# Turning the first pairs' queries and keys at another place in the order of an attention and expert kernel

## The chip, the cores and the metric

One core of a Trainium2 chip runs the whole program. The metric is the device time in microseconds of one execution; the kernel before takes 1123.53 us, the median of three runs that lie between 1121.69 and 1123.55 us. Beside these there is one profiled execution with its trace.

## The reference

Attention with a block causal mask (blocks of 64) over 8 batches, 8 heads, 576 rows and head width 64 is followed by a gated two-layer network on all 4608 rows:

```
scores = scale * (q @ k.T);  scores = where(block_i >= block_j, scores, -1e9)
attn   = exp(scores - max);  attn = attn / (sum + 1e-9);  x = attn @ v
h = x @ w_in                         # 512 -> 2048
out = (h * sigmoid(1.702 * h)) @ w_out   # 2048 -> 512
```

## The kernel before

The attention works on pairs of heads: 32 pairs, four for each batch. The heads of one pair lie on the two halves of the 128 partitions. For each pair a *turn* (`step(n)`) goes through a written list of items, one slot after the other:

- a number such as `1+0`, `2/3` or `4` computes the scores of these row chunks (`score`): matrix products into PSUM banks, then on the vector engine (DVE) a masked minimum at line 351, on the scalar engine (ACT) the exponential with its sum at line 358, then the small DVE operations at lines 368 and 371 (sum plus epsilon, reciprocal), and on GpSimd (POOL) the scaling at line 376;
- `B`, `C` and `a` (`flip`) transpose the scaled weights through the matrix engine (PE, line 102) into a PSUM bank, from which ACT copies them (lines 411 and 424);
- `V` (`av`) multiplies them with the values, and ACT copies the result into `xr` (lines 451 and 450);
- `L` (`prep(n+1)`) turns the queries and the keys of the next pair: two DVE transposes (line 297) from `raw` into `qk`, one of the queries (x = 0) and one of the keys (x = 1), after which `load` issues the eight transfers of a later pair's queries and keys (the one after the next, so that `prep(2)` issues the load of pair 4) on the queue of SP (line 279).

Four pairs form a phase. Turns 0 to 3 use `ORDER[0]`, turn 4 uses `START`, turns 5 to 7 `ORDER[1]` and the rest `ORDER[2]`.

The experts' weights come in 32 pieces of 128 x 512 numbers, split in two by `convert`, which runs a little further after each slot. A piece passes over ACT (line 219), three times over DVE (lines 223, 229, 234), then ACT (line 243) and POOL (line 82); a piece's first ACT step stands behind the last DVE step of the piece before. Its words are loaded by SP (line 202). When the four pairs of the first batch are through, the experts begin on tiles of 384 rows, and from there their matrix products (`hp`, `acc`) are mixed with the attention of later pairs.

The instructions of PE stand in the order in which the program wrote them (`keep_in_program_order`). On the other engines and on the transfer queues a planner in the framework makes the order ahead of time, from its own estimates of durations and landings: where several instructions of an engine are ready by these estimates, the one with the smallest number goes first, and numbers count up in the order of the program. `tc.high_priority(offset=300)` takes 300 from the number. On the chip each engine runs its list in this fixed order and waits at an instruction whose inputs are not there.

A PSUM bank is taken in rotation: until the experts begin there are seven of them, and one turn of the first phase takes 21. The second group of transposes of `B` thus falls on the bank that the last `V` filled, and must wait for the copy at line 451.

Of the kernel before, what the change touches and what calls it, by code (L numbers as in the profile page):

```python
# [23 lines left out]


ORDER = (
# [3 lines left out]
)  # L30
# [10 lines left out]
def attention_moe_kernel(  # L41
# [9 lines left out]
    nc = tc.nc  # L51
    B, H, S, D = q.shape
# [11 lines left out]
    HP = H // 2  # L64
# [9 lines left out]
    def early(n):  # L74

        return n < 2 * HP
# [185 lines left out]
    raw, qk = {}, {}  # L262
# [5 lines left out]
    def load(n):  # L268

        if n in (1, 3):  # L270
            raw[n] = room("xh", [P, 2, S // 32, 32], F32, "raw")
        else:
            raw[n] = d2.tile([P, 2, S // 32, 32], F32, tag="raw", name="raw", bufs=1)
        for x, src in enumerate((q, k)):
            queue = nc.scalar if n < 2 and x else nc.sync
            for hd, b, h in heads(n):
                for c in range(0, D, 32):
                    r = hd * D + c
                    queue.dma_start(
                        out=raw[n][r : r + 32, x],  # L280
                        in_=src[b, h][:, c : c + 32].rearrange("(c p) d -> p c d", p=32),
                    )
# [9 lines left out]
    def prep(n):  # L292

        tag = "e0" if early(n) and n % 2 else "qk"
        qk[n] = d2.tile([P, 2, S], F32, tag=tag, name="qk", bufs=1)
        for x in range(2):
            nc.vector.transpose(out=qk[n][:, x], in_=raw[n][:, x].rearrange("p c d -> p (c d)"))  # L297
        raw.pop(n)
        m = follower(n)
        if m is not None:  # L300
            load(m)
# [154 lines left out]
    def follower(n):  # L456

        m = {0: 2, 1: 3, 2: 4, 3: None}.get(n, n + 1)
        return None if m is None or m >= NPAIR else m
# [4 lines left out]
    def step(n):  # L464

        turns["n"] = n
        now = n < NPAIR

        def item(x):
            if x == "V":  # L470
                return (lambda: av(n - 1)) if n else None
            if x == "L":
                return (lambda: prep(n + 1)) if n + 1 < NPAIR else None
            if x in ("a", "B", "C"):
                m, chunks = {"a": (n, [0, 1]), "B": (n - 1, [2, 3]), "C": (n - 1, [4])}[x]
                return (lambda: flip(m, chunks)) if m >= 0 else None
            return (lambda: score(n, [[int(z) for z in y.split("+")] for y in x.split("/")])) if now and x != "-" else None

        return [item(x) for x in order(n)]
# [139 lines left out]
    load_weights(2)  # L619
    load_v(0)  # L620
    prep(0)
    load_v(1)
    heads_done = 0
# [41 lines left out]
```

## Time and profile before

| | |
|---|---|
| median of three runs | 1123.53 us (1121.69 to 1123.55) |
| profiled execution | 1120.49 us |
| its span, first to last instruction | 1118.6 us |
| mean granted clock of the matrix engine | 0.992 of full speed |
| matrix engine busy over the span | 96% |
| vector engine, scalar engine, GpSimd busy | 52%, 45%, 36% |

The profiled execution is 1.89 us longer than its span and 3.04 us shorter than the median. The busy shares are means over stages that differ: the first 77 us hold the attention of the first batch and the first weights, the rest the experts beside the attention.

### The profile page before, as it was taken

What the parts mean: (1) busy time and instruction counts of PE and PEld (TensorE: products, weight loads), DVE (VectorE), ACT (ScalarE), POOL (GpSimd) and SP (SyncE); (2) the same over time, 40 slices, a digit from 0 to 9 for tenths busy, and PEclk for the clock granted to TensorE, in tenths of its full rate; (3) what the DMA queues carried; (4) which work ended last, traced back from release to release, by engine and by line L of the source; (5) the groups of instructions that cost most, each with busy time, mean ns of one, the idle gap of its engine ahead of it and who ended that gap; (6) DMA issues with size and microseconds to landing.
All of it is one profiled execution on the core that took longest, in us unless ns stands there. A gap on an engine that the chain in (4) does not pass through costs nothing. (4 is left out here: it accounts for less than half of the span.)

```text
span 1118.6 us, 19977 instructions
## 1 busy us (share of the span) xinstructions
PE 1076.4 (96%) x6960; PEld 908.7 (81%) x6960; DVE 583.0 (52%) x1856; ACT 498.6 (45%) x1321; POOL 406.7 (36%) x509
## 2 busy tenths in 40 slices
PE   5969998999999999999999999999999999999998
PEld 3757776788888888888888888888888888899997
DVE  6776885545545555654555655645545654211210
ACT  5866776434534433534443543444434444322322
POOL 4665664333333332333333333333333233122222
PEclk9979999999999999999999999999999999999999
DMA  8734532332444432343443333344342332200000
GB/s 171 205 89 153 150 73 62 84 79 57 105 86 86 103 80 64 64 98 78 98 101 74 75 93 65 70 108 85 81 107 63 71 85 58 54 29 1 29 1 29
DMA packets 219365, 91.25 MB, mean 82 GB/s; under 512 B 197760, under 2 KB 197760, under 8 KB 219264
## 3 DMA queue, kind: packets, MB, share of 16 engines
q1 hardware_dynamic: 214528, 89.38, 34.0%
q10 hardware_dynamic: 4736, 0.59, 0.3%
q8 instruction: 55, 0.90, 0.3%
q14 instruction: 46, 0.38, 0.1%
HBM read 45.09 MB, written 9.44 MB: 49 GB/s over the span
## 5 line engine op out<-in xcount | busy, mean ns | idle before, releaser
L82 POOL TENSOR_TENSOR gl<-g,gh 128x384 fp32r<-128x384 f32 x192 | 194.7, 1014 | 551.5 <-ACT gh L571 449.1
L99 PE MATMUL hp<-xh,wih 128*128 128x384 f32 x768 | 264.7, 345 | 7.9 <-DVE g L563 6.9
L563 DVE SCALAR_TENSOR_TENSOR g<-g,hp 128x384 f32<-128x384 f32 x192 | 105.9, 552 | 319.1 <-ACT g L562 317.8
L99 PE MATMUL hp<-xh,wil 128*128 128x384 f32 x768 | 258.4, 336 | 0.1
L562 ACT ACTIVATE g<-hp 128x384 f32<-128x384 f32 x192 | 94.1, 490 | 359.8 <-PE hp L99 354.8
L99 PE MATMUL hp<-xl,wih 128*128 128x384 f32 x768 | 253.9, 338 | 0.4 <-DVE xl L82 0.4
L99 PE MATMUL acc<-woh,gh 128*128 128x512 f32 x576 | 233.9, 406 | 0.0
L99 PE MATMUL acc<-wol,gh 128*128 128x512 f32 x576 | 226.9, 394 | 0.0
L99 PEld LDWEIGHTS hp<-xh,wih 128*128 128x128 f32 x768 | 144.2, 188 | 34.1 <-DVE g L563 23.1
L99 PE MATMUL acc<-woh,gl 128*128 128x512 f32 x576 | 167.9, 393 | 0.3 <-POOL gl L82 0.3
L571 ACT CAST gh<-g 128x384 fp32r<-128x384 f32 x192 | 98.4, 513 | 156.5 <-DVE g L563 156.4
L99 PEld LDWEIGHTS hp<-xh,wil 128*128 128x128 f32 x768 | 144.3, 188 | 6.5 <-POOL wil L82 0.7
L358 ACT ACTIVATE e<-e,mx 64x64 f32<-64x64 f32 (+4 forms) x240 | 132.3, 552 | 37.6 <-DVE mx L351 37.6
L376 POOL TENSOR_TENSOR e<-e,sm 64x64 f32<-64x64 f32 (+1 forms) x192 | 113.6, 612 | 95.0 <-DVE sm L371 46.5
L99 PEld LDWEIGHTS hp<-xl,wih 128*128 128x128 f32 x768 | 143.6, 188 | 1.3 <-DVE xl L82 1.3
L99 PE MATMUL bank<-qk 64*128 64x320 f32 (+4 forms) x768 | 122.5, 428 | 14.5 <-DVE qk L297 11.1
L99 PEld LDWEIGHTS acc<-woh,gh 128*128 128x128 f32 x576 | 107.9, 187 | 34.2 <-issue 10.5
L99 PEld LDWEIGHTS acc<-woh,gl 128*128 128x128 f32 x576 | 107.8, 188 | 25.9 <-POOL gl L82 1.2
L99 PEld LDWEIGHTS acc<-wol,gh 128*128 128x128 f32 x576 | 108.3, 188 | 16.7 <-POOL wol L82 0.3
L351 DVE CUSTOM_DVE_ANT_0 e<-bank,mask 64x64 f32<-64x64 f32 (+4 forms) x240 | 89.7, 417 | 56.9 <-PE bank L99 52.8
L385 DVE STREAM_TRANSPOSE turned<-e 128x384 f32<-128x384 f32 (+1 forms) x192 | 92.3, 499 | 48.8 <-POOL e L376 48.3
L99 PEld LDWEIGHTS bank<-qk 64*128 64x128 f32 x768 | 69.6, 193 | 54.2 <-issue 25.4
(50 smaller groups left out, 956.0 us busy)
## 6 DMA issues: line engine op xcount, KB each, us to landing
turned<-turned SPq DMA_DIRECT2D x192, 80.0 KB, 2.1
turned<-turned SPq DMA_DIRECT2D x96, 112.0 KB, 2.2
raw<-in_q_dram SPq DMA_DIRECT2D x128, 72.0 KB, 2.4
out_dram<-osb SPq DMA_DIRECT2D x36, 256.0 KB, 2.2
raw<-in_k_dram SPq DMA_DIRECT2D x120, 72.0 KB, 2.6
turned<-turned SPq DMA_DIRECT2D x96, 88.0 KB, 2.1
words<-in_moe_w_in_dram SPq DMA_DIRECT2D x16, 512.0 KB, 6.3
vp<-in_v_dram SPq DMA_DIRECT2D x60, 128.0 KB, 2.4
```

Of the source, the lines that this page charges most:

```text
L82: eng.tensor_tensor(out=out, in0=in0, in1=in1, op=ALU.subtract)
L99: return tc.keep_in_program_order(nc.tensor.matmul(**kw))
L351: nc.vector.tensor_tensor_reduce(out=e[0:m, hd, lo:hi], in0=s, in1=mk, op0=ALU.add, op1=ALU.min, scale=-0.125, scalar=3e38 if lo == 0 else ...
L358: nc.scalar.activation(out=e[0:m, hd], in_=e[0:m, hd], func=AF.Exp, scale=-1.0, bias=mx[0:m, i, hd : hd + 1], accum_out=sm[0:m, i, hd : hd ...
L376: nc.gpsimd.tensor_tensor(out=x, in0=x, in1=sc.to_broadcast([m, width(i)]), op=ALU.mult)
L385: nc.vector.transpose(out=tw[:, :, SLOT[i] : SLOT[i] + i, hd].rearrange("p b j c -> p j b c"), in_=e[:, hd, 0 : i * P],)
L562: nc.scalar.activation(out=g, in_=hp[:, 0:tt], func=AF.Tanh, scale=1.702)
L563: nc.vector.scalar_tensor_tensor(out=g, in0=g, scalar=1.0, in1=hp[:, 0:tt], op0=ALU.add, op1=ALU.mult)
L571: nc.scalar.copy(out=gh, in_=g)
```

## The change

In turns 0 to 3 the item `L` moves from the sixth slot to the third, so that it is written right behind the first scores and a pause, ahead of `B` and `2/3`. In `prep` the two transposes of pairs 0 to 4 are given numbers that are smaller by 300; for the later pairs the offset is 0. The call of `load` behind them keeps ordinary numbers, but is written earlier too. No instruction is added or removed, and the matrix engine's own list is the same.

```diff
 ORDER = (
-    "1+0 - B 2/3 - L C - 4 - V - a -",
+    "1+0 - L B 2/3 - C - 4 - V - a -",
     "1+0 - B - 2 - C - 3 L V - a - 4 -",
     "3+0/2+1 - - - V - - 4 - - - L -",
 )
@@ def prep(n):
         qk[n] = d2.tile([P, 2, S], F32, tag=tag, name="qk", bufs=1)
-        for x in range(2):
-            nc.vector.transpose(out=qk[n][:, x], in_=raw[n][:, x].rearrange("p c d -> p (c d)"))
+
+        with tc.high_priority(offset=300 if n <= HP else 0):
+            for x in range(2):
+                nc.vector.transpose(out=qk[n][:, x], in_=raw[n][:, x].rearrange("p c d -> p (c d)"))
         raw.pop(n)
         m = follower(n)
```

## Rows read from the trace of the kernel before

**Rows 1.** Windows: length, then busy us by engine, PE clock, DMA share, GB/s.

```profile
7.20:76.90 69.70, 55.51 (x472) 40.65 (x472) 55.33 (x198) 54.73 (x168) 43.00 (x58) 0.88 0.67 172
16.40:18.70 2.30, 2.30 (x14) 2.07 (x13) 1.05 (x6) 1.81 (x8) 2.30 (x4) 0.50 0.74 137
60.10:74.00 13.90, 10.04 (x44) 7.01 (x46) 10.73 (x35) 11.67 (x35) 7.52 (x11) 0.51 0.67 173
76.90:200.00 123.10, 112.03 (x775) 89.33 (x776) 87.89 (x243) 80.14 (x208) 71.35 (x76) 1.00 0.37 100
200.00:950.00 750.00, 744.22 (x4850) 630.86 (x4850) 410.33 (x1361) 315.06 (x851) 251.09 (x326) 1.00 0.37 83
```

**Rows 2.** Waits of PE, 7 to 77 us: total us, times, longest us.

```profile
PE bank L99 <- DVE qk L297: 11.1, 4, 7.2
```

**Rows 3.** Timeline of PE: start us, us, instruction, idle before it and releaser.

```profile
15.10 1.41 PE L102 MATMUL bank<-ident,turned 128*128 128x128 f32 x6 [2.16 <-POOL turned L376]
...
32.15 0.76 PE L99 MATMUL bank<-qk 64*128 64x192 f32 x8 [0.58 <-DVE qk L297]
...
43.42 0.76 PE L99 MATMUL bank<-qk 64*128 64x192 f32 x8 [0.79 <-DVE qk L297]
...
58.69 0.76 PE L99 MATMUL bank<-qk 64*128 64x192 f32 x8 [2.52 <-DVE qk L297]
...
63.16 2.37 PE L102 MATMUL bank<-ident,turned 128*128 128x128 f32 x10 [3.12 <-ACT xr L450]
```

**Rows 4.** Timeline of DVE around the transposes of pairs 1 to 4.

```profile
8.71 0.22 DVE L351 CUSTOM_DVE_ANT_0 turned<-bank,mask 64x64 f32<-64x64 f32 x1 [1.53 <-PE bank L99]
...
12.35 0.78 DVE L297 STREAM_TRANSPOSE qk<-raw 128x576 f32<-128x576 f32 x1
...
13.05 0.12 DVE L368 TENSOR_SCALAR sm<-sm 64x2 f32<-64x2 f32 x1
13.09 0.76 DVE L297 STREAM_TRANSPOSE qk<-raw 128x576 f32<-128x576 f32 x1
...
31.14 0.17 DVE L371 RECIPROCAL sm<-sm 128x2 f32<-128x2 f32 x1
31.31 0.78 DVE L297 STREAM_TRANSPOSE qk<-raw 128x576 f32<-128x576 f32 x1
...
42.58 0.78 DVE L297 STREAM_TRANSPOSE qk<-raw 128x576 f32<-128x576 f32 x1
...
54.05 0.53 DVE L351 CUSTOM_DVE_ANT_0 turned<-bank,mask,mx 128x320 f32<-128x320 f32 x1
...
55.11 0.76 DVE L297 STREAM_TRANSPOSE qk<-raw 128x576 f32<-128x576 f32 x1
...
56.38 0.91 DVE L368 TENSOR_SCALAR sm<-sm 128x2 f32<-128x2 f32 x1
...
57.88 0.75 DVE L297 STREAM_TRANSPOSE qk<-raw 128x576 f32<-128x576 f32 x1
```

**Rows 5.** Timeline of SP: the word of piece 4, then the load of pair 4.

```profile
24.24 0.43 SPq L202 DMA_DIRECT2D words<-in_moe_w_out_dram  x1
32.12 1.96 SPq L279 DMA_DIRECT2D raw<-in_q_dram  x4
```

**Rows 6.** Timeline of ACT behind the exponentials of turn 3.

```profile
57.92 0.62 ACT L243 CAST woh<-wm 128x512 fp32r<-128x512 f32 x1 [1.81 <-DVE wm L234]
...
61.35 0.62 ACT L243 CAST woh<-wm 128x512 fp32r<-128x512 f32 x1 [2.29 <-DVE wm L234]
...
62.44 0.58 ACT L451 COPY xr<-bank 128x512 f32<-128x512 f32 x1
```

**Rows 7.** Single lines, whole span: duration ns min/median/max, first and last start.

```profile
L297 DVE STREAM_TRANSPOSE qk<-raw x64: 730/769/779, 5.7 to 917.5; 128x576 f32<-128x576 f32 x64
L368 DVE TENSOR_SCALAR sm<-sm x160: 117/169/1197, 13.0 to 950.3; 128x2 f32<-128x2 f32 x128, 64x2 f32<-64x2 f32 x32
```

**Rows 8.** Timeline of POOL beside the 0.91 us operation of line 368.

```profile
55.45 1.81 POOL L376 TENSOR_TENSOR turned<-turned,sm 128x448 f32<-128x448 f32 x2
```

## The prediction, written before the change was run

> **What bounds the kernel now.** I read the windows first, because the busy shares of the whole span mix stages. From 200 to 950 us the matrix engine (PE) is busy 744.22 of 750 us [rows 1]: nothing done on the vector engine (DVE) can shorten that. From 76.9 to 200 us it is busy 112.03 of 123.10. In the first stage, 7.2 to 76.9 us, it is busy 55.51 of 69.70, so 14.2 us are idle, and DVE (55.33) and ACT (54.73) are as busy as PE [rows 1]: three engines wait for each other in turn. PE's list is fixed and the experts behind 76.9 us are bound by it, so what the first stage saves or loses is passed on nearly whole to the end. That stage is all this change touches.
>
> Second, PE's waits there: 11.1 us are for the turned queries and keys, in four waits [rows 2]. The longest, 7.2, is the first load from memory and stays; three are left, 0.58, 0.79 and 2.52 us, at the first scores of turns 2, 3 and 4 [rows 3], together 3.89 us. Behind the last one PE soon stops again, 3.12 us, until ACT has copied the result of the last `V` [rows 3]. At the start there is a wait of 2.16 us for POOL's scaling [rows 3].
>
> Third, the list of DVE, to see why the transposes are late. A transpose takes 0.77 us and never more than 0.78 [rows 7], so its cost isn't in question, only its place. In turn 3 the queries' transpose (55.11) stands behind the minimum of chunk 4 at 54.05, and the keys' (57.88) behind line 368 of chunk 4 at 56.38 [rows 4]. Both are written in the ninth slot, later than `L` in the sixth, so they had the larger numbers and yet went first. The same holds for pair 2, whose keys (31.31) stand behind line 371 of chunk 4 at 31.14 [rows 4]; pair 3 at 42.58 repeats it. An instruction overtaken by larger numbers wasn't ready by the planner's estimate: its data had not landed there. The queue in front of it is not the whole reason, then, and a smaller number alone should not move pairs 2 to 4 much. Pair 1 (12.35, 13.09) is not shown to be held so.
>
> **The change part by part.** No instruction is added, so every price is one of place.
>
> *Pair 1, smaller numbers.* Its two transposes lie before and after line 368 at 13.05 [rows 4], which with line 371 feeds the scaling that PE awaits until 15.10 [rows 3]. DVE is idle for 1.53 us before its first minimum at 8.71 [rows 4], nearly room for both (1.54 us). Moved there they give line 368 up to 0.70 us (13.05 less 12.35), and the reciprocal the second 0.76 as well: 0 to 1.46 us. The lower bound holds if the data lands too late and DVE stands still for what it saves later. I take 0.9, a little over half, as the gap is there but the landing unknown.
>
> *Pairs 2 and 3.* By the order argument they stay where they are: 0 taken, with bounds of 0 and 0.58 + 0.79 = 1.37 us. Where they do move forward, the 1.5 us of each pair go in front of minima and small operations which ACT awaits; the cover is that the same 1.5 us leave the place just before the next scores. Without that cover a pair costs up to 1.5.
>
> *Pair 4, by way of the transfer queue.* `L` in the third slot is written ahead of the word of piece 4, which is loaded by the `convert` of that same slot; before, that word went at 24.24 and pair 4's load followed at 32.12 [rows 5]. Now the load has the smaller number. On the chip nothing is lost by it: the load still waits for the second transpose of pair 2 (31.31) [rows 4, 5], the word waits behind it, and piece 4 is needed by DVE only after 54 us. In the planner's estimate, however, pair 4 lands one word earlier, and piece 4 later by the load of pair 4, whose two halves stand 57.88 less 55.11 = 2.77 us apart [rows 4]: about 5.5 us for both, an estimate. So the keys should be turned before the last exponentials of turn 3, and the 2.52 us wait goes.
>
> What is late next is the copy at line 451, for which PE waits 3.12 us [rows 3]. It was done only at 62.44, behind two pieces' ACT steps at 57.92 and 61.35 that themselves stand still 1.81 and 2.29 us for DVE [rows 6]. One piece takes 61.35 less 57.92 = 3.43 us there. If the order of ACT stays, PE merely waits 5.6 us in one place rather than in two, and nothing is won: lower bound 0. If piece 4 starts a piece later in the plan, one piece less stands ahead of the copy: 3.43 us. If both go behind it, the copy could come where ACT stood still ahead of the first, at 57.92 less 1.81 = 56.1 [rows 6], 6.3 us earlier. I take 2.6, three quarters of a piece, because its first ACT step may still be in front.
>
> [...]
>
> *Later pairs* have the offset 0: nothing.
>
> *A term that speaks against any reordering of DVE.* Line 368 takes 0.169 us in the median, but up to 1.197 [rows 7]; the one at 56.38 takes 0.91 and ends, at 57.29, where POOL's scaling ends, 55.45 + 1.81 = 57.26 [rows 4, 8]. The transposes show no such stretch. [...] Each time the new order sets such an operation against a POOL operation it costs up to 1.197 less 0.169 = 1.03 us, and gains as much where it parts them; the sum takes 0 for it, with 1.0 either way.
>
> Sum: 0.9 + 0 + 2.6 + 0 = 3.5 us less. The profiled execution took 1120.49 us and would take 1117.0. The median of the runs is 3.04 us above that execution, so 1123.53 becomes 1120.0 us, 0.3% less.
>
> **The rivals.**
>
> [...]
>
> *The wait only changes its place (1122.5).* The transposes go earlier, but the copy at line 451 stays behind two pieces: pair 4's 2.52 us are added to the 3.12. Only pair 1's 0.9, or little more, is left. For it: rows 6 show ACT held by DVE's weight work, which nothing here shortens. This holds too where the planner moves nothing but pair 1.
>
> *Slower (1126).* ACT's order ahead of line 451 gets worse. If DVE, freed of the transposes in 55 to 58 us, lets the plan fit a third piece in front of the copy, PE waits 3.43 us longer; with 0.9 won at pair 1 that is 2.5 more. It decides from the point where three pairs of lines 243 and 219 stand before line 451. Against it: with its word later, piece 4 should start later.
>
> **How the numbers follow.** A difference under 0.2%, 2.2 us, is about what measuring this kernel can't tell from none. My forecast (2.2 to 5.5 us won, its own range 1118 to 1121.3) has 0.35; all waits gone 0.20; the wait in another place, with a gain or loss under 2.2 us, 0.27; slower 0.18. Hence faster 0.55, same 0.27, slower 0.18. The likeliest gives 1120.0. For eight in ten, the range goes from 1114, which holds most of the clock's case, to 1126, the slower case; beyond lie an early copy together with the whole 5.0 us, and two stretched operations on top of a third piece.
>
> **What would show it.** Right: PE's waits for line 297 at turn 4 gone; pair 4's load ahead of piece 4's word in SP's list; line 451 of pair 2 with one piece fewer before it; the first `hp` product 3 to 4 us earlier than 76.9. Wrong: the transposes of pairs 2 and 3 more than 3 us earlier against the work around them (then the number did decide); the copy still behind two pieces; or idle time after 76.9 us grown by what was won, if later weight pieces come too late.

## The result, and the profile of the changed kernel

The changed kernel is slower by a fifth of a per cent: 1126.24 us in the median of 22 runs (1122.10 to 1127.04), beside 1122.97 us for the kernel before in 22 runs on the same chips (1121.69 to 1124.98). The ratio to the kernel before is 1.0021 with a 95% interval of 1.0014 to 1.0029, that is about 2.4 us (the medians lie 3.3 us apart; how the single times spread is told at the end, and the text goes by the ratio). The forecast was 1120.0 us and faster; the median stands just above 1126, the top of its range, on the other side of no change. (By the ratio, 1123.53 becomes 1125.9 us, just under it.) The profiled execution took 1124.02 us with a span of 1122.1 us, 3.5 us more than before.

In the rows of after the lines of `prep` and of what follows stand two higher than before: the transposes are line 299 (were 297), the minima 353, the exponentials 360, the sum's and the reciprocal's operations 370 and 373 (were 368 and 371), the scaling 378, the copies into `xr` 453 and 452 (were 451 and 450). Lines 202, 219 to 243 and 279 are unchanged.

The windows come first, in the columns of [rows 1]:

```profile
7.20:76.90 69.70, 53.26 (x464) 39.20 (x464) 54.70 (x196) 53.77 (x164) 40.63 (x55) 0.88 0.66 171
60.10:74.00 13.90, 7.93 (x49) 5.48 (x50) 10.46 (x33) 10.59 (x31) 6.50 (x9) 0.63 0.81 213
76.90:200.00 123.10, 112.95 (x746) 89.87 (x748) 88.61 (x232) 80.22 (x206) 71.48 (x77) 0.97 0.37 100
200.00:950.00 750.00, 742.62 (x4874) 630.03 (x4868) 411.68 (x1365) 314.54 (x851) 252.15 (x328) 1.00 0.37 83
```

PE got through less in the first stage (53.26 us where [rows 1] show 55.51), and from 200 to 950 us it is about as full as before, 742.62 of 750 us. The loss is in the first 200 us. PE's waits from 7 to 77 us, answering to [rows 2], name the place:

```profile
PE bank L99 <- DVE qk L299: 10.6, 4, 7.3
PE bank L102 <- ACT xr L452: 6.0, 1, 6.0
```

The waits for turned queries and keys, which the change is about, fell from 11.1 to 10.6 us. The wait for the copy grew to 6.0. The timeline of PE shows the same waits one by one, as in [rows 3]:

```profile
15.52 1.79 PE L102 MATMUL bank<-ident,turned 128*128 128x128 f32 x6 [3.32 <-POOL turned L378]
...
32.96 0.76 PE L99 MATMUL bank<-qk 64*128 64x192 f32 x8 [0.58 <-DVE qk L299]
...
44.23 0.76 PE L99 MATMUL bank<-qk 64*128 64x192 f32 x8 [0.79 <-DVE qk L299]
...
58.84 0.76 PE L99 MATMUL bank<-qk 64*128 64x192 f32 x8 [1.87 <-DVE qk L299]
...
66.17 2.37 PE L102 MATMUL bank<-ident,turned 128*128 128x128 f32 x10 [5.97 <-ACT xr L452]
...
78.76 0.45 PE L99 MATMUL hp<-xh,wih 128*128 128x384 f32 x1 [0.71 <-ACT xr L452]
```

Turns 2 and 3 wait the same 0.58 and 0.79 us as before; turn 4 waits 1.87 where it waited 2.52; and the wait behind it is 5.97 us where it was 3.12. The experts begin at 78.76 us, before at 76.91: 1.85 us later. Why the copy is late, ACT's timeline answers, beside [rows 6]:

```profile
56.71 0.60 ACT L219 ACTIVATE wm<-words 128x512 f32<-128x512 f32 x1
60.94 0.62 ACT L243 CAST woh<-wm 128x512 fp32r<-128x512 f32 x1 [3.62 <-DVE wm L234]
...
64.36 0.62 ACT L243 CAST woh<-wm 128x512 fp32r<-128x512 f32 x1 [2.29 <-DVE wm L234]
...
65.44 0.58 ACT L453 COPY xr<-bank 128x512 f32<-128x512 f32 x1
```

The same two pieces stand in front of the copy as before, pieces 4 and 5, but they begin later. The products that the copy takes had ended on PE at 56.17 us (before at 55.36): ACT stood 3.62 and 2.29 us at line 243, with the copy behind it in its list. Piece 4's first step (line 219) stood ahead of turn 3's last two exponentials, as ACT's timeline of before has it:

```profile
53.25 0.66 ACT L219 ACTIVATE wm<-words 128x512 f32<-128x512 f32 x1
...
54.45 0.80 ACT L358 ACTIVATE turned<-turned,mx 128x576 f32<-128x576 f32 x1
```

Now it stands behind them, at 56.71. DVE shows what that costs, beside [rows 4]:

```profile
12.35 1.43 DVE L299 STREAM_TRANSPOSE qk<-raw 128x576 f32<-128x576 f32 x2
13.71 0.19 DVE L370 TENSOR_SCALAR sm<-sm 64x2 f32<-64x2 f32 x2
...
14.16 0.22 DVE L373 RECIPROCAL sm<-sm 64x2 f32<-64x2 f32 x2
...
15.70 1.61 DVE L370 TENSOR_SCALAR sm<-sm 128x2 f32<-128x2 f32 x1
...
53.34 0.77 DVE L299 STREAM_TRANSPOSE qk<-raw 128x576 f32<-128x576 f32 x1
...
56.83 0.97 DVE L370 TENSOR_SCALAR sm<-sm 128x2 f32<-128x2 f32 x1 [1.28 <-ACT turned L360]
57.84 0.17 DVE L373 RECIPROCAL sm<-sm 128x2 f32<-128x2 f32 x1
58.01 0.78 DVE L299 STREAM_TRANSPOSE qk<-raw 128x576 f32<-128x576 f32 x1
58.72 0.67 DVE L223 TENSOR_SCALAR wm<-wm 128x512 uint32<-128x512 uint32 x1
```

In the kernel before, DVE used the time in which ACT made the last exponentials for the first two of its three steps of piece 4:

```profile
54.51 0.69 DVE L223 TENSOR_SCALAR wm<-wm 128x512 uint32<-128x512 uint32 x1
...
55.80 0.66 DVE L229 SCALAR_TENSOR_TENSOR wm<-words,wm 128x512 uint32<-128x512 uint32 x1
```

Now it stands idle for 1.28 us at that point, as its list has no step of piece 4 there any more, and line 223 follows only at 58.72: 4.2 us later, of which 0.8 had come up before (the table below). The queries of pair 4 went earlier (53.34, before 55.11), the keys did not (58.01, before 57.88). The queue of SP, beside [rows 5], shows where it started:

```profile
32.93 1.96 SPq L279 DMA_DIRECT2D raw<-in_q_dram  x4
34.93 2.12 SPq L279 DMA_DIRECT2D raw<-in_k_dram  x4
37.09 0.97 SPq L202 DMA_DIRECT2D words<-in_moe_w_out_dram  x2
```

Pair 4's load stands ahead of the word of piece 4, the first of the two at 37.09; before, that word went at 24.24. It is issued by 38 us, and 12 such transfers landed in 5.5 us in the median, so on the chip it should be there long before 56.71 (an estimate from these two). That it is late in the planner's estimate, and that this sets the order of ACT and DVE, is argued from the lists: no run prints the planner's estimates. Word back, below, shows that the word's place decides. The same happened once more: pair 5's load now stands ahead of the word of piece 11.

Where the 3.5 us between the two profiled executions arose can be read from the copies into `xr` (128x512), as PE's list is the same in both kernels:

| copy of pair | before | after | difference | added since the copy above |
|---|---|---|---|---|
| 0 | 30.72 | 31.52 | 0.80 | 0.80 |
| 1 | 42.07 | 42.89 | 0.82 | 0.02 |
| 2 | 62.44 | 65.44 | 3.00 | 2.18 |
| 3 | 76.15 | 78.01 | 1.86 | -1.14 |
| 4 | 115.61 | 116.18 | 0.57 | -1.29 |
| 5 | 144.46 | 146.61 | 2.15 | 1.58 |
| 6 | 172.22 | 174.27 | 2.05 | -0.10 |
| 7 | 200.87 | 204.72 | 3.85 | 1.80 |

The 2.18 us are the late copy. Behind pair 3 ACT's order differs as well, so that the copy of pair 4 measures PE badly: PE began the products ahead of it at 111.96 us before and at 113.24 after, 1.28 us apart, where the copies are 0.57 apart. What moves the difference between pairs 3 and 5 was not taken apart; in after the clock fell to 0.50 from 80 to 82 us, in before it did not. The last step, between pairs 6 and 7, is the hand-over to the second phase. There both kernels have the same wait of 2.00 us for POOL, and what differs is the clock granted behind it (first after, then before; windows and PE's timeline):

```profile
192.00:194.00 2.00, 2.00 (x7) 2.00 (x7) 0.73 (x2) 1.35 (x4) 0.00 (x0) 0.50 0.00 0
...
190.62 1.20 PE L102 MATMUL bank<-ident,turned 128*128 128x128 f32 x9 [2.00 <-POOL turned L378]
```

```profile
192.00:194.00 2.00, 1.50 (x13) 0.89 (x10) 1.74 (x11) 1.50 (x7) 0.00 (x0) 1.00 0.02 4
...
188.30 1.20 PE L102 MATMUL bank<-ident,turned 128*128 128x128 f32 x9 [2.00 <-POOL turned L376]
```

0.50 is the lowest clock that a window of 2 us shows in either execution between 6 and 206 us; at it one product of 128x384 took 0.53 us, at 1.00 it took 0.33 (after, 80 to 82 and 84 to 86 us). Nine of the twelve profiled executions have this fall, four kernels without the moved slot among them (number alone, copy first, turned ahead and both ahead; see the end), so it can't be counted as a cost of the change.

### The profile page after: what moved, and what is told of

The parts are those of the page before. It is cut to its first block, busy times and chain, and to the rows that moved or that the text cites. A ratio compares the mean times of both kernels' runs of the same rounds, so it can differ in the third digit from the quotient of the medians.

```text
span 1122.1 us, 19978 instructions
## 1 busy us (share of the span) xinstructions
PE 1077.1 (96%) x6960; PEld 909.8 (81%) x6960; DVE 586.5 (52%) x1856; ACT 499.4 (45%) x1321; POOL 406.5 (36%) x509
## 5 line engine op out<-in xcount | busy, mean ns | idle before, releaser
L99 PE MATMUL bank<-qk 64*128 64x320 f32 (+4 forms) x768 | 121.1, 427 | 12.8 <-DVE qk L299 10.6
```

The costliest lines, as they stand in the source:

```text
L99: return tc.keep_in_program_order(nc.tensor.matmul(**kw))
```

## The experiments

The theory was: the cost is ACT's order ahead of the copy of pair 2, made by pair 4's load having gone ahead of piece 4's word. Its measure is the distance from pair 1's copy to pair 2's, which is free of what happened earlier: 20.37 us before, 22.55 after. The rivals: that the smaller numbers, and so the order of DVE, cost it; and that the loss lies elsewhere. Every kernel was timed in five rounds against the kernel before on its chip.

**Slot alone.** The order of items is the change's, all numbers are ordinary.

```diff
-        with tc.high_priority(offset=300 if n <= HP else 0):
+        with tc.high_priority(offset=0):
```

> Only the third slot for L, ordinary numbers. Theory (the load of pair 4 ahead of piece 4's word sets ACT's order): the transfer list and ACT's list are those of the changed kernel, so the copy of pair 2's result (line 451 of before) comes 2 to 3 us later than 62.44, while the copy of pair 0 stays at 30.7; ratio 1.0010 to 1.0020. Rival (the transposes' own new places cost the time): no loss, ratio 0.9995 to 1.0005.

Measured: 1125.07 us, ratio 1.001 (1.000 to 1.002); the distance is 22.56, PE waits 5.98 us for the copy. The whole shift of the copy comes from the slot. The ratio is at the lower edge of the range of the theory, and its interval reaches into that of the rival, so that it is the distance that decides. The copies' own times missed: pair 0's, expected at 30.7, came at 33.15, and pair 2's at 66.42, 4.0 us after 62.44. PE's products for `V` of pair 0 show most of it. They took 4.64 us where before, at a granted clock of 1.00, they took 2.98:

```profile
28.56 4.64 PE L99 MATMUL bank<-turned,vp 128*64 128x128 f32 x60 [1.58 <-ACT turned L413]
```

Word back and first swap only have them as long (4.64 and 4.63 us); that the clock had fallen there is an estimate from these lengths. The distance leaves it out.

**Number alone.** The order of items is that of before, the transposes keep their smaller numbers.

```diff
-    "1+0 - L B 2/3 - C - 4 - V - a -",
+    "1+0 - B 2/3 - L C - 4 - V - a -",
```

> Only the smaller numbers, L in the sixth slot as before. Theory: only DVE's list changes; pair 1's second transpose delays line 368 of turn 0 by 0.7 us, the copy of pair 0 comes 0.8 us later than 30.72 and the copy of pair 2 by no more than that; ratio 1.0003 to 1.0010. Rival (the transposes' places cost the time): the whole loss, ratio 1.0015 to 1.0029.

Measured: 1124.67 us, ratio 1.0004 (0.9994 to 1.0014); the distance is 20.37 as before. The numbers move DVE's list at pair 1 and at pair 4, whose queries now stand ahead of line 223 (54.94, then 55.64) in place of behind it. They do not move the copy: pair 0's is 0.41 us later than before (0.8 was expected) and pair 2's 0.43.

**Word back.** The change, with the word of piece 4 loaded together with that of piece 3, and so ahead of pair 4's load.

```diff
-                    load_weights(j + 3)
+                    load_weights(j + 4 if j == 1 else j + 3)
```

> The changed kernel, but the word of piece 4 is loaded one piece earlier, so that it stands ahead of pair 4's load again. Theory: the copy of pair 2 comes back to 62.4 to 63.3 us and PE's wait for it from 5.97 to 3 to 3.5; what is left is pair 1's 0.8, ratio 1.0003 to 1.0010. Rival (later weight pieces, whose words are also behind a load, cost the time after 77 us): ratio stays at 1.0015 to 1.0025.

Measured: 1122.6 us, ratio 0.9986 (0.9975 to 0.9997). The distance is 20.37 again, and the timelines of PE and of ACT show the wait of before and piece 4's first step in its old place, ahead of the exponentials. (The copy itself, expected at 62.4 to 63.3, is at 64.52, as pair 0's is late here too.)

```profile
65.24 2.36 PE L102 MATMUL bank<-ident,turned 128*128 128x128 f32 x10 [3.12 <-ACT xr L452]
```

```profile
55.33 0.65 ACT L219 ACTIVATE wm<-words 128x512 f32<-128x512 f32 x1
...
64.52 0.58 ACT L453 COPY xr<-bank 128x512 f32<-128x512 f32 x1
```

One word's place in a transfer queue thus made the whole shift of the copy, and with it back the interval of the ratio lies below the change's. The ratio came out lower than expected, below 1; this kernel keeps the second swap, pair 5's load ahead of piece 11's word, and its lists of ACT and DVE differ from those of before behind 77 us.

**First swap only.** To part the two swaps: the change with pair 5's load in its old place. The new item `D`, in the slot in which `L` stood before, issues in turn 3 alone the load that `prep(4)` leaves out.

```diff
-    "1+0 - L B 2/3 - C - 4 - V - a -",
+    "1+0 - L B 2/3 D C - 4 - V - a -",
...
         raw.pop(n)
+        if not (n == 4):
+            load_next(n)
+
+    def load_next(n):
         m = follower(n)
...
+            if x == "D":
+                return lambda: load_next(n + 1) if (n + 1) == 4 else None
```

> The change with one of its two swaps on the transfer queue undone: pair 5's load stands behind piece 11's word again, as before; pair 4's load stays ahead of piece 4's word. Theory: the first swap carries the whole cost and the second pays a part back, as the kernel with the second swap alone (word_back) hints by 0.9986 against 1.0004 for the numbers alone. Then the copy of pair 2 stays 22.4 to 22.7 us behind that of pair 1, PE waits 5.5 to 6.5 us for it, and the ratio to before is 1.003 to 1.0045, above the change's own 1.0021. Rival: the second swap does nothing and word_back's gain was chance: the same 22.4 to 22.7 us, but a ratio of 1.001 to 1.0025.

Measured: 1124.26 us, ratio 1.0015 (1.0004 to 1.0025). The distance is 22.55, PE waits 5.5 us. The theory's 1.003 was wrong, the rival's range held: beside the first swap the second does nothing that these runs can tell from none (1.0015 against 1.0021). Why word back was below 1 stays open.

**Copy first.** The kernel before, with one edit: piece 4's second ACT step (line 243) and all that follows in the pieces is put behind the copy of pair 2, so that line 243 of neither piece stands ahead of it.

```diff
         while conv["step"] < int(2 * upto):
+            if conv["step"] == 9 and "copy" not in conv:
+                load_weights((int(2 * upto) - 1) // 2 + 3)
+                return
...
-            if odd:
+            if conv["step"] == 9:
+                with tc.issue_after(conv["copy"]):
+                    split_weights(j)
+                    load_weights(j + 3)
+                    begin(j + 1)
+            elif odd:
                 split_weights(j)
...
-        nc.scalar.copy(out=xr[:, h, c0 + BLK : c0 + S], in_=o)
+        last = nc.scalar.copy(out=xr[:, h, c0 + BLK : c0 + S], in_=o)
+        if n == 2:
+            conv["copy"] = last.ins
```

> The kernel before, but the second half of piece 4 and what follows it is queued on ACT behind the copy of pair 2's result. Theory (that copy's place on ACT is what the matrix engine stands for in turn 4): the copy comes at 56 to 58 us instead of 62.44, PE's wait of 3.12 us goes, ratio 0.9945 to 0.9975. Rival (another wait on DVE or POOL takes its place, since these are as busy as PE up to 77 us): ratio 0.998 to 1.001.

Measured: 1119.93 us, ratio 0.9957 (0.9943 to 0.9970). ACT's timeline:

```profile
53.45 0.64 ACT L219 ACTIVATE wm<-words 128x512 f32<-128x512 f32 x1
...
56.19 0.57 ACT L461 COPY xr<-bank 128x512 f32<-128x512 f32 x1
...
58.11 0.62 ACT L243 CAST woh<-wm 128x512 fp32r<-128x512 f32 x1 [1.24 <-DVE wm L234]
```

The copy comes 6.25 us earlier than before, the distance is 13.92, and PE's wait for it is gone, though the keys' wait of 2.52 us stays. The theory's range held.

**One piece first.** The same edit with step 11 in place of 9, so that one piece stands ahead of the copy.

> The kernel before, with the copy of pair 2's result behind one piece's ACT steps instead of two. Theory (each piece ahead of the copy costs about 3.4 us of waiting): the copy comes at 58.5 to 60 us, PE's wait for it is under 1 us, ratio 0.9960 to 0.9985, between none and two pieces. Rival (the edit wins by delaying the weights and not by the copy): as with no piece ahead, 0.9945 to 0.9965.

Measured: 1119.83 us, ratio 0.9966 (0.9954 to 0.9978); the copy is at 59.20, the distance 16.94. With two, one and no pieces ahead the copy comes at 62.44, 59.20 and 56.19, and the ratio is 1, 0.9966 and 0.9957: about 3.1 us of the copy's time for each piece. The first piece taken away brought 0.0034; the second's 0.0009 is within the intervals. The theory had the copy's time right; the ratio lies in its range and only 0.0001 outside the rival's, so it does not part the two. PE waits 1.9 us here for a later copy on ACT (line 421), which stands behind the second piece.

**Change and copy first.** The edit of copy first, on the changed kernel.

> The changed kernel with the copy of pair 2's result queued ahead of piece 4's second half on ACT. Theory (the loss comes through ACT's order): the copy comes at 56.5 to 58 us, PE's wait of 5.97 us for it goes, and the kernel lies within 0.001 of the kernel before with the same edit (0.9957), so 0.9945 to 0.9970. Rival (the change costs its time elsewhere as well): 0.998 or more.

Measured: 1121.26 us, ratio 0.9981 (0.9972 to 0.9990). The wait for the copy is gone here as well, but the kernel is 0.0024 behind copy first. The rival held: the copy is not all that the change costs. In the profiled executions the other parts are 0.6 us up to the copy of pair 1 (0.2 of them the first load, the rest told below), about 0.45 us in turn 3, where piece 4's first step (56.69) now stands directly ahead of the copy, and 1.8 us between the copies of pairs 3 and 5, where the products of 128x384 from 79.7 to 80.6 us took 0.52 us and in copy first took 0.33. DVE still gets piece 4 late (line 243 follows at 60.93, in copy first at 58.11).

**Turned ahead.** The kernel before, with the keys' transposes where the change wanted them: line 368 of chunk 4 in turns 0 to 3 is put behind the next pair's keys.

```diff
+            conv["keys", n] = nc.vector.transpose(out=qk[n][:, x], in_=raw[n][:, x].rearrange("p c d -> p (c d)")).ins
...
+        with tc.issue_after(conv["keys", n + 1]) if n < HP and i == NCH - 1 else ExitStack():
+            nc.vector.tensor_scalar(
...
```

> The kernel before, with the keys' transposes of pairs 1 to 4 forced ahead of the small operation of chunk 4 (line 368) on DVE; ACT's and SP's lists stay. Theory: PE's waits of 0.58, 0.79 and 2.52 us for the keys shrink to under 1.5 in all, but the copy of pair 2 keeps its place behind two pieces, so PE's wait for it grows by about what turn 4 gains; ratio 0.9980 to 1.0005. Rival (the waits for the keys are worth their length): 3 us or more are won, ratio 0.9975 or less.

Measured: 1123.76 us, ratio 1.0006 (0.9998 to 1.0015). PE's waits from 7 to 77 us:

```profile
PE bank L99 <- DVE qk L299: 7.2, 1, 7.2
PE bank L102 <- POOL turned L379: 2.9, 1, 2.9
PE bank L102 <- ACT xr L453: 2.7, 1, 2.7
...
PE bank L99 <- DVE sm L371: 1.7, 1, 1.7
PE bank L99 <- DVE mx L353: 1.6, 1, 1.6
```

All 3.89 us of waits for `qk` are gone, only the first load's is left. Nothing is won: a wait of 1.7 us for `sm` has come in, those for `mx` and for POOL have grown to 1.6 and 2.9 us (0.9 and 2.2 before), and the copy is still waited for. That last wait was expected to grow and is 2.7 us, not 3.1. The upper end of the expected ratio was missed by 0.0001, and the rival's 0.9975 is out.

**Both ahead.** The edits of copy first and of turned ahead together, on the kernel before.

> Both: the copy ahead on ACT and the keys' transposes ahead on DVE, on the kernel before. Theory: with the copy no longer behind it, the shorter wait for the keys pays; 1 to 2.5 us less than the copy alone, ratio 0.9930 to 0.9950. Rival (DVE's minima take the place of the wait): the same as the copy alone, 0.9950 to 0.9965.

Measured: 1117.14 us, ratio 0.9946 (0.9934 to 0.9958), the lowest of all. The copy is at 56.22. The theory's range held, but the intervals of this kernel and of copy first (0.9957) overlap. In the profiled executions the way from the copy of pair 1 to that of pair 3 is 27.43 us here, 29.47 in copy first, 33.31 in turned ahead and 34.08 before: there the keys' places are worth 2.0 us with the copy ahead, and 0.8 without. Part of it may be the clock, which was 0.61 from 60 to 64 us in copy first and 1.00 from 60 to 66 us here.

**Change and both ahead.** The same two edits on the changed kernel.

> The change with both edits of both_ahead: piece 4's split and what follows behind the copy of pair 2, and line 370 of chunk 4 in turns 0 to 3 behind the next pair's keys' transpose. Theory: with both orders set by hand nothing of the change's damage in turns 1 to 4 is left, and what its lists cost elsewhere (0.0024 between the two kernels with the copy edit alone) shrinks to that of pair 1: 0.9945 to 0.9965, PE waiting under 1 us for that copy. Rival: the change costs the same 0.0024 here as well, beyond turn 4: 0.9965 to 0.998.

Measured: 1120.86 us, ratio 0.9982 (0.9972 to 0.9992). The theory was wrong and the rival came near: 0.0036 lie between the two, more than the 0.0024. The windows from 56 to 78 us, with both ahead first, then change and both ahead:

```profile
56.00:78.00 22.00, 15.23 (x130) 11.66 (x129) 18.74 (x48) 15.16 (x45) 14.73 (x17) 1.00 0.45 113
```

```profile
56.00:78.00 22.00, 15.35 (x119) 11.48 (x117) 17.36 (x48) 16.32 (x47) 13.88 (x17) 0.84 0.53 137
```

DVE got 1.4 us less work done there on the changed kernel. DVE's timeline of change and both ahead, from just ahead of that stretch, shows one reason (its lines 307, 361 and 379 are the transposes, minima and sum operations):

```profile
52.92 0.77 DVE L307 STREAM_TRANSPOSE qk<-raw 128x576 f32<-128x576 f32 x1
...
53.66 1.03 DVE L379 TENSOR_SCALAR sm<-sm 128x2 f32<-128x2 f32 x1
54.61 0.41 DVE L361 CUSTOM_DVE_ANT_0 turned<-bank,mask 128x256 f32<-128x256 f32 x1
...
57.31 0.52 DVE L379 TENSOR_SCALAR sm<-sm 128x2 f32<-128x2 f32 x1 [0.59 <-ACT turned L368]
```

Pair 4's queries now stand ahead of minima for which ACT waits, a small operation grew to 1.03 us there, and the copy came at 57.74, 1.5 us later than in both ahead. PE waits only 0.33 us for it, though, as expected. Its long wait has moved to a later copy on ACT, that of line 422 (PE's timeline, then ACT's):

```profile
62.10 0.75 PE L102 MATMUL bank<-ident,turned 128*64 128x128 f32 x4 [2.79 <-ACT turned L422]
```

```profile
60.18 0.62 ACT L243 CAST woh<-wm 128x512 fp32r<-128x512 f32 x1 [1.76 <-DVE wm L234]
...
61.68 0.36 ACT L422 COPY turned<-bank 128x256 f32<-128x256 f32 x1
```

That copy stands behind piece 4's line 243, and piece 4 is still late on DVE (line 223 at 57.95, in both ahead at 54.74). The edit took the copy of pair 2 out from behind the late piece, but not that later one. The experts begin at 73.04 us, in both ahead at 70.66.

## Why the prediction was wrong

**The stage and its bound were right.** The changed lists touch the first stage, and what it loses reaches the end: PE is as full from 200 to 950 us as before.

**Pairs 2 and 3, taken at 0: right.** They did not move against the work around them, and their waits are the same 0.58 and 0.79 us. The reason given, that an instruction overtaken by larger numbers was not ready by the planner's estimate, fits number alone, where 300 off the number moved nothing there; the planner's estimates themselves are not on record.

**Pair 1, taken at 0.9 us won: wrong in sign.** The transposes did not go into the gap before the first minimum. Both went directly in front of line 370 (12.35, then 13.71), where before only one had, and the first reciprocal went from 13.78 to 14.16. From the first transpose of the run to POOL's first scaling it is 8.16 to 8.32 us in the six kernels without the smaller numbers, and 8.64 to 8.73 in the six with them: about 0.4 us lost. The lower bound was given as 0, "DVE stands still for what it saves later"; that a transpose could step in front of the operations that POOL waits for was not weighed. Number alone has this and one step at pair 4, and its ratio of 1.0004 can't be told from 1.

**Pair 4, taken at 2.6 us won: the step that failed.** The forecast had the swap on SP right, and that piece 4 would move back in the plan. It then said that "one piece less stands ahead of the copy". None did, which the prediction itself had named as a sign of being wrong. Piece 4 came later, but still before the copy, with piece 5 behind it. (The 5.5 us by which piece 4 should land later in the plan came from places in DVE's list; no run shows it, and what moved is ACT's first step of piece 4, by 3.5 us.) What was lost is the cover: DVE's steps of piece 4 had lain in the wait for ACT's exponentials and now follow it. The term measured +2.2 us at the copy in place of -2.6, of which 1.1 came back by the copy of pair 3 (the table). The sentence that the keys would be "turned before the last exponentials" failed with it: they stay behind lines 370 and 373, and 0.65 us of the 2.52 went.

**The rival "slower" had the place and not the mechanism.** It named ACT's order ahead of line 451 and 1126 us, and let it decide by a third piece in front of the copy. Two were enough, 3 us later, so that its 1126 us, near the measured 1126.24, is luck. Its argument against, that piece 4 starts later, was in fact the cause.

**The clock is open in the change and plain beside it.** It has the last 0 of the sum, and the range counts it at up to 5.0 us, the whole of which lies beyond its lower end. No run shows that figure; what the runs show is the granted clock itself, and a product of 128x384 that took 0.53 us at 0.50 and 0.33 at 1.00. From 60.1 to 74 us the granted clock is 0.51 to 0.63 in the kernels in which PE stops there for the copy (before, after, slot alone, number alone, word back, turned ahead, first swap only), and 0.76 to 1.00 in the five in which piece 4 or 5 was put behind the copy. The case of all waits gone, which the chances give 0.20, came nearest in another kernel: both ahead took 1117.14 us with the clock at 1.00 there, and the longest wait from 10 to 77 us is 2.0 us. The change alone is no way to it.

**The stretched small operation, taken at 0 with 1.0 either way, went against.** The longest is now 1.61 us, above the 1.197 that the bound went by [rows 7]. It lies beside a scaling on POOL:

```profile
14.47 2.82 POOL L378 TENSOR_TENSOR turned<-turned,sm 64x64 f32<-64x64 f32 x6 [11.25 <-DVE sm L373]
```

It runs from 15.70 to 17.31, POOL's six operations from 14.47 to 17.29. Number alone and word back, which have the smaller numbers too, have it at 1.62 us; before, slot alone and copy first, which do not, have 0.51 at that place. What it cost by itself was not measured apart.

Together: the pieces tried alone (1.0004 for the numbers, 1.001 for the slot) add up to 1.0014, and the change has 1.0021 (1.0014 to 1.0029); the rest is within the intervals. How much of the change's 2.4 us is the late copy, and how much falls of the clock that came or did not come in an execution, is open: the profiled pair has the experts begin 1.85 us later.

## What to carry to other kernels

Where a planner fixes the order ahead of time from its own estimates, moving one transfer moves work on engines that it never touches: read the queue of the transfers, name what is overtaken in it, and ask which engine's list was filled with that late work and what it covered. A wait removed from an engine that has another wait right behind it is worth nothing until the second is gone; here the copy behind the conversions was the one to move. The transposes alone won nothing (1.0006); that they pay once the copy is out of the way is what the profiled executions show, while the times can't tell 0.9946 from 0.9957. To compare kernels whose executions differ by chance, measure between two events that the same lists lead up to, here from copy to copy, and not from the span's start.

## What the hardware showed unexpectedly

The clock falls behind the same stop in one execution and not in another. At the hand-over, behind the same 2.00 us wait, it was 0.50 in after and 1.00 in before. From pair 5's copy to pair 7's it is 55.9 to 56.6 us in three of the twelve executions (before, word back and one piece first), 57.4 in first swap only and 58.0 to 58.4 in the other eight. At the start the mean clock over 13 to 25 us was 0.86 in four executions and 0.72 in eight; slot alone, whose DVE list is that of before until turn 1, has 0.72, and before has 0.86. Between 72 and 85 us the products of 128x384 took 0.52 or 0.53 us in place of 0.33 in all six kernels with the moved slot and, of the six without it, only in one piece first; in after the granted clock was 0.50 there (80 to 82 us); with one execution each, whether the change makes that likelier is open.

The single times show the same from the other side. They spread from 1121.7 to 1125.0 us for the kernel before and from 1122.1 to 1127.0 for the changed one, and the order goes largely by the mean granted clock that is on record with each run: the nine runs of the changed kernel from 1122.1 to 1124.9 us have 0.989, the thirteen from 1125.4 to 1127.0 have 0.986 to 0.988. Of the 29 runs of the kernel before that stand beside slot alone, the eight with 0.986 took 1124.7 to 1126.4 us and the sixteen with 0.989 or more 1120.3 to 1124.0. One profiled execution thus can't decide over 0.2%.

An operation on 128x2 numbers, 0.17 us in the median, took 1.61 us beside running POOL operations and ended within 0.02 us of the last of them. The two minima ahead of it, which run beside the same row of POOL operations, kept their length: 0.54 and 0.53 us, as in the kernel before.
